# Lightning attention into a top-1 mixture of experts: token lists built on the chip by one-hot products, attention steps in three array shapes, ordered masks, and first loads by half heads

## The chip, the cores and the metric

The kernel runs on one core of a Trainium2 chip. A core has TensorE (PE, with a separate queue for its weight loads, PEld), VectorE (DVE), ScalarE (ACT), GpSimd (POOL) and SyncE (SP, which issues transfers here), an on-chip SBUF, and the matmul accumulators PSUM in eight banks. The metric is device microseconds of one execution, lower is better. Times are medians of several runs; durations inside the kernel come from one profiled execution.

## The reference

Everything is fp32. `q`, `k`, `v` have the shape (B, H, S, D) = (4, 8, 768, 64); `lam` has one decay per head. The second half has N = B x S = 3072 tokens of 512 features, E = 8 experts and F = 1024 hidden features.

```python
# attention, per 64-position block, with a state (D x D) per batch and head
intra = (q_blk @ k_blk.T) * Dmask            # Dmask[i, j] = lam ** (i - j) for i >= j, else 0
out_blk = intra @ v_blk + (q_blk * lam ** (pos + 1)) @ kv_state
kv_state = lam ** 64 * kv_state + (k_blk * lam ** (63 - pos)).T @ v_blk
...
x = out.transpose(0, 2, 1, 3).reshape(B * S, H * D)     # 3072 x 512
# top-1 mixture of experts
logits = x @ w_gate
expert = argmax(logits, axis=1)
gate = softmax probability of that expert
for e in range(E):
    xe = x[expert == e]
    out[expert == e] = gate * (relu(xe @ w1[e]) @ w2[e])
```

## The kernel before

**Attention.** The kernel uses chunks of 128 positions (NSTEP = 6 of them) in place of the 64 of the reference, which gives the same result. One step handles one chunk `n` of two batches; `order` is the list of the twelve steps, (0, 0), (0, 2), (1, 0), and so on. While a step is finished, the next one is prepared. The parts of a step are:

- `turn_q` and `turn_k` (L216, L228) transpose q and k on PE into `tq` and `tk` (the two halves s = 0 and 1 hold four heads each); ACT copies them to SBUF; DVE makes `qsT`, the q scaled for the state (L224), and POOL makes `kd`, the decayed k (L238).
- `score` (L243) multiplies k and q per head into PSUM banks `sp`; DVE multiplies them with the decay matrix into `mt` (L254).
- `attend` (L282) multiplies `mt` with v into `op`; `attend_states` (L265) adds what comes from the running state `st`, in two goes (`way` 0 and 1).
- `grow` (L296) makes the new contribution `cp` to the state; `update` (L308) adds it, after POOL has decayed the old state (`sd`, L316).
- `rows` (L320) transposes the result with identity columns and gate weights side by side (`back`) into `tx`, so that the rows of x and the gate logits come out of one product; ACT copies both, and x is written to a DRAM array `xs`.

**Routing.** `choose` (L338) takes the largest logit of each token, makes a one-hot `oh` of its expert and keeps the running counts `acc`. `put` (L370) computes with two products (`rank`) where each token stands in its expert's list, and POOL scatters an entry (row in `xs`, row in the output, gate value) for each token into a DRAM array `slots`, 128 tokens by one indirect transfer (L390, 24 in all). `slots` was filled with empty entries at the start. This is done for groups of four batches (512 tokens) for the first four chunks, and of two for the last two.

**Experts.** Expert 0 comes first, in two passes: 256 tokens gathered early ("0a", from `start_early`, L685 on) while attention still runs, then the rest ("0b"). The other seven follow in an order sorted by their counts. A pass loads its list from `slots` (L412), gathers its rows of `xs` (L436), transposes them (`tp`, L465), multiplies with w1 (`ph`, L475, or the faster form `hidden_fast`, `p`, L551) and w2 (`po`, L609, and `p`, L579), and scatters the rows to the output (L442). Weights, 2 MB of w1 and 2 MB of w2 per expert, are loaded by SP, double buffered. ACT and DVE share the copies out of PSUM: the transposed rows (`xgT`, L450 and L452), the hidden layer with its relu (`hT`), and the outputs `o`. When the early group has its counts (`acc_early`), the product `had` (L688) tells how many of expert 0's tokens there are by then, so that the places of later tokens start behind the 256 of the early pass. A small ACT copy, `fence` (L280), keeps attend from writing the `op` banks while the states' products still do.

**Order.** Where the code says `pin` (`tc.keep_in_program_order`), the instructions keep the order of the program among themselves; all other instructions are placed by the framework's scheduler. All matmuls of the steps are pinned. PSUM banks are shared: `sp`, `tq`, `tk` in 0 to 3; `cp` in 4; `rank` and `had` in 5; `op` in 6 and 7; `tx` of the first batch of a step in 4 and 5, of the second in 6 and 7. The order of PE in a step is `leave(last)` (its eight `tx` products), the turns of the next step, `rank` where a group is due, states way 0, `cp`, attend, states way 1, and the next step's scores. These are several shapes of use of the array (rows x columns): 128x128 for `tx` and turns, 64x64 for states, 128x64 for `cp` and attend, 64x128 for scores.

Of the kernel before, what the change touches and what calls it, by code (L numbers as in the profile page):

```python
# [20 lines left out]
def kernel(  # L21
# [28 lines left out]

    nc = tc.nc
# [4 lines left out]
    P = 128  # L56
# [7 lines left out]
    TG = 3  # L64
    NR = E - 1
# [5 lines left out]
    CUT = B // 2  # L71
# [10 lines left out]

    xs = dram.tile([1 + N, MD], F32, name="xs")
# [4 lines left out]

    def load(n, b0, first=False):

        got = [qkv.tile([P, 2, H, D], F32, tag=name, name=f"{name}_in") for name in "qkv"]
        per = 1 if first else 2
        for t, src in zip(got, (q, k, v)):
            queue = nc.scalar if first and src is k else nc.sync
            for b in range(0, 2, per):
                queue.dma_start(
                    out=t[:, b:b + per].rearrange("p b h d -> p (b h) d"),
                    in_=src[b0 + b:b0 + b + per, :, n * C:(n + 1) * C, :].rearrange(
                        "b h s d -> s (b h) d"))
            if first and src is q:  # L100
                load_lam()
        return got
# [3 lines left out]

    def load_lam():
        nc.sync.dma_start(out=lam_bc, in_=lam.partition_broadcast(P))

# [12 lines left out]
    for j, u in itertools.product(range(2), range(2)):  # L122
        nc.scalar.dma_start(out=back[(u ^ j) * D:((u ^ j) + 1) * D, :, P + j * E:P + (j + 1) * E],
                            in_=by_chunk[j, u])
# [21 lines left out]
    for i in range(E):  # L146
        nc.vector.memset(caps[:, i:i + 1], float(CAPS[i]))

    entry = const.tile([P, NSTEP, B, ENTRY], F32, name="entry")
    nc.gpsimd.memset(entry, 0.0)  # L150
    nc.gpsimd.iota(entry[:, :, :, 0].bitcast(I32), pattern=[[B * C, NSTEP], [C, B]], base=1,
                   channel_multiplier=1)
    nc.gpsimd.iota(entry[:, :, :, 1].bitcast(I32), pattern=[[C, NSTEP], [S, B]], base=0,
                   channel_multiplier=1)
# [23 lines left out]
    def load_weights(e):  # L178
        w1t = wpool.tile([P, DC, F], F32, tag="w1", name="w1t")
        nc.sync.dma_start(out=w1t, in_=pick(w1_r, e))  # L180
        w2t = wpool.tile([P, FC, MD], F32, tag="w2", name="w2t")
        nc.sync.dma_start(out=w2t, in_=pick(w2_r, e))
# [21 lines left out]
    def pin(inst):  # L204
        tc.keep_in_program_order(inst)


    turned_shape = [P, HP // 2, 2, C]

    def turned(src, s, t):  # L210
        for i, b in itertools.product(range(HP // 2), range(2)):
            h = s * HP + 2 * i
            pin(nc.tensor.transpose(t[:, i, b, :], src[:, b, h:h + 2, :], ident))  # L213
# [29 lines left out]
    def score(m, s):  # L243
# [3 lines left out]
        for i, b, u in itertools.product(range(HP // 2), range(2), range(2)):  # L247
            pin(nc.tensor.matmul(  # L248
                sp[u][:, i, b, :], lhsT=m.kT[s][halves[u], i, b, :], rhs=m.qT[s][halves[u], i, b, :],
                start=(i == 0 and b == 0), stop=(i == HP // 2 - 1 and b == 1),  # L250
                skip_group_check=True))
        mt = work.tile([P, 2, HP // 2, 2, C], F32, tag="mt", name="mt")
        for u in range(2):
            nc.vector.tensor_mul(  # L254
                mt[:, u], sp[u],
                decay[:, u, s * HP // 2:(s + 1) * HP // 2].unsqueeze(2).to_broadcast(shp))
        m.mt.append(mt)

    fence = const.tile([P, 1], F32, name="fence")
# [4 lines left out]

    def attend_states(m, way):  # L265

        if way == 0:
            m.op = [bank(6 + b, [P, HP, C], f"op{b}") for b in range(2)]
        if m.n > 0:
            for hp, b in itertools.product(range(HP), range(2)):  # L270
                u = b ^ way
                pin(nc.tensor.matmul(  # L272
                    out_at(m, b, u, hp), lhsT=st[halves[u], m.b + b, hp, :],
                    rhs=m.qsT[hp // 2][halves[u], hp % 2, b, :],
                    start=(way == 0 and hp < 2), stop=(way == 1 and hp >= HP - 2),
                    skip_group_check=True))
        if m.n > 0 and way == 0:


            nc.scalar.copy(fence[halves[0]], out_at(m, 1, 1, HP - 1)[:, C - 1:])  # L280

    def attend(m):  # L282
        for hp, b, u in itertools.product(range(HP), range(2), range(2)):
# [568 lines left out]
```

## Time and profile before

| what | value |
|---|---|
| median of 3 runs | 479.15 us (478.34 to 479.39) |
| profiled execution, its own time | 478.98 us |
| its span, first to last instruction | 477.2 us |
| mean granted TensorE clock | 0.997 |
| bytes moved by DMA | 72.84 MB, mean 153 GB/s |

The span has three parts. Attention with routing lasts to about 131 us, the first expert's early pass overlaps its end, and the passes of the experts fill the rest, to the last scatter. A line of the timeline view reads: start, length, engine, source line, operation, output and inputs by the program's names, shape of the array use, sizes, count, and in brackets the engine's idle time before it and what ended that. Durations of matmuls overlap, since they are pipelined, so the distance between two starts tells the cost. A line of the windows view gives the window, its length, the busy time and number of instructions of PE, PEld, DVE, ACT and POOL, the granted clock, the busy share of DMA, and the GB/s.

### The profile page before, as it was taken

Reading aid. Unit: us, or ns where it says so; the run is one execution under the profiler, and the core shown is the slowest. Engines: PE = TensorE matmul, PEld = TensorE weight load, DVE = VectorE, ACT = ScalarE, POOL = GpSimd, SP = SyncE. Lnnn points to the kernel's source line nnn. Section 1 sums busy time; section 2 is a strip of 40 time slices with the busy share of each in tenths; the row PEclk is TensorE's granted clock in tenths of the full one; section 3 lists DMA queues with packets and bytes.
Section 4 is the critical chain, followed back from the end, with each engine's and each line's share of the span. In section 5 each row is a group of like instructions: output and inputs, shape, how many; then the busy total and the mean of one; then the engine's idle time right before and its main releaser. Section 6 shows DMA issues by size and latency. Waiting matters only on the chain.

```text
span 477.2 us, 8695 instructions
## 1 busy us (share of the span) xinstructions
PE 457.3 (96%) x3468; PEld 383.1 (80%) x3468; DVE 224.4 (47%) x525; ACT 127.0 (27%) x323; POOL 247.7 (52%) x189
## 2 busy tenths in 40 slices
PE   4799999999899999999999999999999999999994
PEld 3789999998686677957994898699699689779963
DVE  3657758585450134452345436434524623753421
ACT  3364445544320111222131122113112212211310
POOL 5423644524335829849806951991694497711001
PEclk9999999999999999999999999999999999999998
DMA  9999999999318557060506152351633615001001
GB/s 170 240 243 260 217 239 216 257 305 279 101 47 320 157 193 250 32 243 33 208 13 242 36 212 87 157 199 47 243 110 132 233 39 211 0 19 44 1 17 51
DMA packets 99856, 72.84 MB, mean 153 GB/s; under 512 B 81226, under 2 KB 81230, under 8 KB 99808
## 3 DMA queue, kind: packets, MB, share of 16 engines
q1 hardware_dynamic: 88688, 51.97, 39.2%
q0 software_dynamic: 5008, 13.41, 7.8%
q10 hardware_dynamic: 6112, 6.83, 4.3%
q8 instruction: 29, 0.48, 0.5%
q14 instruction: 19, 0.16, 0.1%
HBM read 59.13 MB, written 13.40 MB: 152 GB/s over the span
## 4 chain that ended last, share of the span: by engine, by line
PE 71%; issue 3%; DVE 1%; DMA 1%; POOL 0%; POOLq 0%; ACT 0%
PE p L551 28%; PE p L579 18%; PE po L609 16%; PE ph L475 5%; PE tp L465 3%; DMA xg<-xs,list_0a 1%; DVE h_qsT L498 0%; DVE hT L560 0%; PE tx L326 0%; POOL slots L390 0%; PE tx L328 0%; DVE xgT L452 0%; PE rank L377 0%; POOLq L805 0%; ACT hT L562 0%
## 5 line engine op out<-in xcount | busy, mean ns | idle before, releaser
L609 PE MATMUL po<-w2t,hT 128*128 128x512 f32 (+2 forms) x224 | 81.1, 597 | 0.0
L436 POOL DMA_INDIRECT xg<-xs,list x24 | 26.0, 1084 | 75.7 <-PE tp L465 70.2
L609 PEld LDWEIGHTS po<-w2t,hT 128*128 128x128 f32 (+2 forms) x224 | 31.6, 169 | 37.5 <-issue 37.2
L562 ACT ACTIVATE hT<-hT 128x384 f32<-128x384 f32 (+2 forms) x56 | 30.2, 540 | 89.8 <-DVE hT L560 89.8
L442 POOL DMA_INDIRECT out_dram<-o,list x24 | 23.7, 989 | 52.0 <-DVE o L615 28.9
L551 PE MATMUL p<-xgT,w1t 128*128 128x192 f32 (+2 forms) x224 | 42.8, 334 | 0.0
L390 POOL DMA_INDIRECT slots<-entry,slot_i x24 | 23.6, 985 | 34.9 <-DVE slot_i L388 13.7
L551 PEld LDWEIGHTS p<-xgT,w1t 128*128 128x128 f32 x224 | 38.7, 190 | 1.1 <-issue 0.8
L238 POOL TENSOR_TENSOR kd<-k_in,kdec 128x512 f32<-128x512 f32 x20 | 20.4, 1042 | 26.5 <-PE cp L301 14.7
L254 DVE TENSOR_TENSOR mt<-sp,decay 128x512 f32<-128x512 f32 x48 | 29.8, 682 | 6.2 <-PE sp L248 6.1
L591 DVE SCALAR_TENSOR_TENSOR o<-p,list,o 128x256 f32<-128x256 f32 x28 | 13.5, 483 | 32.9 <-PE p L579 17.0
L579 PE MATMUL p<-w2t,hT 128*128 128x256 f32 x112 | 26.8, 382 | 0.0
L579 PEld LDWEIGHTS p<-w2t,hT 128*128 128x128 f32 x112 | 21.0, 190 | 6.9 <-issue 4.4
L248 PE MATMUL sp<-qT,kT 64*128 64x128 f32 x384 | 24.7, 278 | 0.1
L248 PEld LDWEIGHTS sp<-qT,kT 64*128 64x128 f32 x384 | 22.4, 188 | 2.2 <-issue 1.9
L284 PE MATMUL op<-mt,v_in 128*64 128x128 f32 x384 | 23.6, 274 | 0.4 <-ACT fence L280 0.4
L475 PE MATMUL ph<-xgT,w1t 128*128 128x256 f32 (+1 forms) x128 | 23.9, 342 | 0.0
L560 DVE TENSOR_TENSOR hT<-p,u_qsT 128x384 f32<-128x384 f32 (+2 forms) x28 | 16.1, 575 | 16.5 <-PE p L551 16.5
L213 PE MATMUL tq<-ident,q_in 128*128 128x128 f32 x96 | 15.4, 286 | 7.9 <-DMA q_in<-in_q_dram 6.8
L465 PEld LDWEIGHTS tp<-ident,xg 128*128 128x128 f32 (+1 forms) x112 | 13.4, 140 | 11.7 <-issue 3.6
L293 ACT COPY xT<-op 128x512 f32<-128x512 f32 x24 | 12.9, 590 | 33.6 <-PE op L272 29.8
L488 DVE TENSOR_TENSOR u_kT<-p,u_qT 128x384 f32<-128x384 f32 (+2 forms) x14 | 8.1, 576 | 29.3 <-PE p L551 29.3
(162 smaller groups left out, 968.5 us busy)
## 6 DMA issues: line engine op xcount, KB each, us to landing
w1t<-in_moe_w_dram SPq DMA_DIRECT2D x8, 2048.0 KB, 7.7
w2t<-in_moe_w_dram SPq DMA_DIRECT2D x8, 2048.0 KB, 9.1
xs<-x ACTq DMA_DIRECT2D x24, 256.0 KB, 4.8
q_in<-in_q_dram SPq DMA_DIRECT2D x11, 512.0 KB, 8.4
k_in<-in_k_dram SPq DMA_DIRECT2D x11, 512.0 KB, 8.4
v_in<-in_v_dram SPq DMA_DIRECT2D x11, 512.0 KB, 8.7
q_in<-in_q_dram SPq DMA_DIRECT2D x2, 256.0 KB, 5.9
k_in<-in_k_dram ACTq DMA_DIRECT2D x2, 256.0 KB, 5.6
```

Of the source, the lines that this page charges most:

```text
L248: pin(nc.tensor.matmul(sp[u][:, i, b, :], lhsT=m.kT[s][halves[u], i, b, :], rhs=m.qT[s][halves[u], i, b, :], start=(i == 0 and b == 0), st ...
L254: nc.vector.tensor_mul(mt[:, u], sp[u], decay[:, u, s * HP // 2:(s + 1) * HP // 2].unsqueeze(2).to_broadcast(shp))
L284: pin(nc.tensor.matmul(out_at(m, b, u, hp), lhsT=m.v[:, b, 2 * hp + u, :], rhs=m.mt[hp // 2][:, u, hp % 2, b, :], start=(m.n == 0 and hp = ...
L390: put = nc.gpsimd.indirect_dma_start(out=slots, out_offset=bass.IndirectOffsetOnAxis(ap=slot_i[:, i:i + 1], axis=0), in_=entry[:, n, b, :] ...
L436: nc.gpsimd.indirect_dma_start(out=dst, out_offset=None, in_=xs[:rows, :], in_offset=bass.IndirectOffsetOnAxis(ap=idx, axis=0))
L442: put = nc.gpsimd.indirect_dma_start(out=out, out_offset=bass.IndirectOffsetOnAxis(ap=idx, axis=0), in_=src, in_offset=None, bounds_check= ...
L465: pin(nc.tensor.transpose(tp[:, t * P:t * P + w], m.xg[t // 2][:w, t % 2, dc * P:(dc + 1) * P], ident[:w, :w]))
L475: nc.tensor.matmul(ph, lhsT=w1t[:, dc, fc * P:(fc + 1) * P], rhs=m.xgT[:, dc, :], start=(dc == 0), stop=(dc == DC - 1))
L551: nc.tensor.matmul(p[:, i, :], lhsT=lhs[:, dc, (c + i) * P:(c + i + 1) * P], rhs=rhs[:, dc, :], start=(dc == 0), stop=(dc == DH - 1))
L562: nc.scalar.activation(outs[i][k], outs[i][k], ACT.Relu)
L579: nc.tensor.matmul(p, lhsT=lhs[:, fc, :], rhs=rhs[:, fc, :], start=(fc == 0), stop=(fc == FC // 2 - 1))
L609: nc.tensor.matmul(po[part], lhsT=m.hT[:, fc, t * P:t * P + w], rhs=w2t[:, fc, :], start=(i < k), stop=(i >= FC - k), skip_group_check=True)
```

## The change

Four things are changed together.

1. **Lists on chip.** `put` becomes `place` and `fill`. `place` computes each token's spot in the lists as before (the DVE array that was called `place` is now `spots`, and reads `rank` first), then splits it into the tile of the list (spot >> 7) and the lane (spot & 127). DVE compares an iota with the lane to make a one-hot matrix `to` (128x128), and puts token row and gate into the column of the tile in `what` (128x64). `fill` multiplies the two on PE into `new` (bank 5), and DVE adds that to `lists` in SBUF. No entry is scattered to DRAM, `slots` isn't emptied at the start, and no list is loaded; row numbers for the gathers and the output are worked out by DVE in `rows_of`. The lists of the seven sorted experts are picked by products with `is_r` (`by_turn`). The scatter to `slots` is kept in a branch that runs only where an expert gets more tokens than the passes hold. Chunk 4 is now grouped by four batches too, so there are seven groups (five of 512 tokens, two of 256), and the early pass takes tokens of chunks 0 to 3.
2. **Three array shapes.** The score products are halved in columns, to 64x64. The order of PE in a step becomes: `rank` where due, turns of half 0 and `tx` of the first batch, turns of half 1 and `tx` of the second, `cp`, attend, `fill` where due, states way 0, scores, states way 1.
3. **Masks and update ordered.** The masks (`mask`, the product with the decay) and the update of the state are kept in program order on DVE: mask of half 0, update, mask of half 1. `sd` on POOL is issued ahead of `cp`.
4. **First loads.** q and k of the first step are loaded by halves of the heads, on SP and ACT; gate weights and `lam` go to POOL's queue; all loads on SP keep the program's order, with the first weights ahead of the last v.

The core of the diff:

```diff
+        if first:
+            for hs, b, i in itertools.product((slice(0, HP), slice(HP, H)), range(2), range(2)):
+                (nc.sync, nc.scalar)[i].dma_start(
+                    out=got[i][:, b, hs],
+                    in_=(q, k)[i][b0 + b, hs, where, :].rearrange("h s d -> s h d"))
...
+            if (n, b0) == (NSTEP - 1, B - 2) and src is v:
+                weights.append(load_weights(0))
...
-    def load_lam():
-        nc.sync.dma_start(out=lam_bc, in_=lam.partition_broadcast(P))
+    nc.gpsimd.dma_start(out=lam_bc, in_=lam.partition_broadcast(P))
...
-        for i, b, u in itertools.product(range(HP // 2), range(2), range(2)):
-            pin(nc.tensor.matmul(
-                sp[u][:, i, b, :], lhsT=m.kT[s][halves[u], i, b, :], rhs=m.qT[s][halves[u], i, b, :],
+        for i, b, u, keys in itertools.product(range(HP // 2), range(2), range(2), halves):
+            in_order(nc.tensor.matmul(
+                sp[u][keys, i, b, :], lhsT=m.kT[s][halves[u], i, b, keys],
+                rhs=m.qT[s][halves[u], i, b, :],
...
-        for i, b in enumerate(bs):
-            put = nc.gpsimd.indirect_dma_start(
-                out=slots, out_offset=bass.IndirectOffsetOnAxis(ap=slot_i[:, i:i + 1], axis=0),
-                in_=entry[:, n, b, :], in_offset=None)
+        nc.vector.tensor_single_scalar(parts_i[:, 0], spot, 7, op=ALU.arith_shift_right)
+        nc.vector.tensor_single_scalar(parts_i[:, 1], spot, P - 1, op=ALU.bitwise_and)
...
+            nc.vector.tensor_scalar(out=to[:, i], in0=lane, scalar1=parts[:, 1, i:i + 1],
+                                    scalar2=None, op0=ALU.is_equal)
+            nc.vector.scalar_tensor_tensor(
+                out=what[:, i],
+                in0=tiles_of.rearrange("p e t -> p (e t)").unsqueeze(2).to_broadcast(shp),
+                scalar=parts[:, 0, i:i + 1],
+                in1=entry[:, n, b].unsqueeze(1).to_broadcast(shp),
+                op0=ALU.is_equal, op1=ALU.mult)
...
+        new = bank(5, [P, E * NT * 2], "new")
+        for i, half in itertools.product(range(len(bs)), halves):
+            mm = nc.tensor.matmul(
+                new[half], lhsT=to[:, i, half], rhs=what[:, i].rearrange("p c k -> p (c k)"),
+                start=(i == 0), stop=(i == len(bs) - 1), skip_group_check=True)
...
     for i in range(len(order)):
-        due = chosen.pop() if chosen else None
-        if last:
-            leave(last)
+        give_places()
         ahead = enter(*order[i + 1]) if i + 1 < len(order) else None
...
+            for s in range(2):
+                if ahead:
+                    turn_q(ahead, s)
+                    turn_k(ahead, s)
+                leave(last, s)
+            grow(cur)
+            attend(cur)
+            fill_lists()
         attend_states(cur, 0)
-        grow(cur)
-        attend(cur)
...
         if ahead:
             for s in range(2):
                 score(ahead, s)
+            mask(ahead, 0)
+        else:
+            turn(passes[0], in_order)
+            give_places()
+        attend_states(cur, 1)
+        if i > 0:
+            to_sbuf(cur)
+            update(cur)
+        if ahead:
+            mask(ahead, 1)
```

## The prediction

> **What bounds the kernel now.** I read the head of the page first, for the busy time of each engine and the chain that ended last:
>
> ```profile
> span 477.2 us, 8695 instructions
> PE 457.3 (96%) x3468; PEld 383.1 (80%) x3468; DVE 224.4 (47%) x525; ACT 127.0 (27%) x323; POOL 247.7 (52%) x189
> PE   4799999999899999999999999999999999999994
> PE 71%; issue 3%; DVE 1%; DMA 1%; POOL 0%; POOLq 0%; ACT 0%
> ```
>
> TensorE is busy for 457.3 of 477.2 us, so it is idle for 19.9 in all: the first two slices, one place near slice 10, one of 1.05 us at 414, and the last scatter of some 6.5 us. Time changes only where PE's own work changes, or where PE waits. I therefore read PE's timeline next, in an undisturbed step (columns: start, length, operation, count):
>
> ```profile
> 62.85 0.60 PE L213 MATMUL tq<-ident,q_in 128*128 128x128 f32 x4
> 64.60 0.31 PE L377 MATMUL rank<-oh,before 128*128 128x32 f32 x2
> 65.06 0.67 PE L272 MATMUL op<-qsT,st 64*64 64x128 f32 x16
> 65.66 1.15 PE L301 MATMUL cp<-v_in,kd 128*64 128x64 f32 x32
> 66.64 1.92 PE L284 MATMUL op<-mt,v_in 128*64 128x128 f32 x32
> 68.49 0.67 PE L272 MATMUL op<-qsT,st 64*64 64x128 f32 x16
> 69.09 2.06 PE L248 MATMUL sp<-qT,kT 64*128 64x128 f32 x32
> 71.07 0.50 PE L326 MATMUL tx<-back,xT 128*128 128x136 f32 x2
> ...
> 73.03 0.60 PE L213 MATMUL tq<-ident,q_in 128*128 128x128 f32 x4
> ...
> 80.88 0.50 PE L326 MATMUL tx<-back,xT 128*128 128x136 f32 x2
> ```
>
> Starts are what to read, since ends overlap: a step takes 80.88 - 71.07 = 9.81 us, and one with a rank 71.07 - 60.90 = 10.17, together 19.98 per pair of steps. PE never pauses here. Then the same view at the start and where attention hands over to the experts, where the bracket names the wait:
>
> ```profile
> 7.23 1.76 PE L213 MATMUL tq<-ident,q_in 128*128 128x128 f32 x7 [1.94 <-DMA q_in<-in_q_dram]
> 15.75 0.63 PE L213 MATMUL tk<-ident,k_in 128*128 128x128 f32 x4 [1.45 <-DMA k_in<-in_k_dram]
> 109.34 0.39 PE L688 MATMUL had<-acc_early,ones 128*128 128x8 f32 x2 [0.27 <-DVE place L383]
> 117.25 1.75 PE L284 MATMUL op<-mt,v_in 128*64 128x128 f32 x28 [0.18 <-ACT fence L280]
> 125.65 1.75 PE L284 MATMUL op<-mt,v_in 128*64 128x128 f32 x28 [0.20 <-ACT fence L280]
> 129.53 0.55 PE L465 MATMUL tp<-ident,xg 128*128 128x128 f32 x3 [1.27 <-DMA xg<-xs,list_0a]
> ```
>
> Last the stage windows (busy PE, PEld, DVE, ACT, POOL, then clock, DMA share, GB/s), and DVE's timeline where a POOL product runs beside it:
>
> ```profile
> 0.00:20.00 20.00, 10.55 (x128) 9.35 (x128) 7.54 (x29) 5.84 (x10) 9.84 (x29) 1.00 1.07 203
> 80.00:100.00 20.00, 20.00 (x330) 18.52 (x328) 13.78 (x36) 9.82 (x32) 10.11 (x10) 1.00 1.03 282
> 96.23 0.17 DVE L367 TENSOR_TENSOR acc<-acc,oh 128x8 f32<-128x8 f32 x1
> 96.43 0.92 DVE L366 COPY ohc<-acc 128x8 f32<-128x8 f32 x1
> ```
>
> In the steps DVE is 69% busy and the transfers fill their share; in the first 20 us PE is half idle while the DMA engines are full. The 0.92 us for a copy that elsewhere takes 0.17 falls inside a `kd` product on POOL (96.28 to 97.32). All of it ran at clock 1.00, so no term below needs a clock.
>
> **The changes on PE.** From about 137 us the experts' passes are the same products; the sum concerns what lies before. Inside a block, by the raw starts of the matmuls, a transpose costs 0.109 us, a `tx` 0.2325, four 64x64 passes together 0.109, a `cp` pair 0.058, an attend pair 0.109, two score passes 0.112. A step's work is thus 8 x 0.2325 + 16 x 0.109 + 2 x 0.436 (states) + 0.933 (cp) + 1.747 (attend) + 1.787 (score) = 8.95; the other 0.86 of 9.81 are five changes of array shape. The score products are halved in columns: twice the instructions, 64 passes, four at once as the states' passes show, 16 x 0.109 = 1.74; should they be limited by the rate of issue that the `cp` stream shows (14.6 ns each, 128 instructions), 1.87. I take 1.74, since the states have the same form. Three shapes instead of five leave about 0.50 for changes (0.42 to 0.60), so a step becomes about 8.91 + 0.50 = 9.41, 0.40 less. Against this stands `fill`: two products of two passes per 128 tokens, priced by attend's passes, 0.117; a group of four 0.47. A pair of steps is then 2 x 9.41 + 0.47 + 0.36 to 0.46 (rank) = 19.65 to 19.75, or 0.30 less; over five pairs -1.5, and with one rank pair fewer at the end against two small fills, -1.6. With scores at 1.87 it is -0.2.
>
> **Waits that go.** The lists are on chip, so 24 indirect scatters on POOL (985 ns each, 23.6 us busy), the filling of the empty list (0.44 MB), and seven list loads on SP go. On PE's path that frees the gather wait: the early tokens now end one step group sooner and their gather is issued at about 112, ahead of the turn at 128. 1.27 + the two fence waits 0.38 + had's old 0.27 = -1.9. Released gathers and the first weights move past each other on SP and POOL: v of the last step is then behind 4 MB of weights and lands at some 113, needed at 123, so nothing is paid; if that cover went, each us late is a us of PE. The 0.30 for `xgT` stays, as 0.4.
>
> **The start.** q and k come in halves on two queues, so the first score can start at 7 rather than 10.5. But PE then runs into k of the second step, which needs 8 loads x 0.524 = 4.19 MB. Transfers begin at 2.1 us; the first window's 203 GB/s x 20 us is 4.06 MB in 17.9 us, 0.227 MB per us, and 4.19 MB end at 20.6, up to 1 us more for the tail (a list load of 6 KB takes 3.4 from issue to landing, so not all of a transfer is bytes). With the fullest slice's rate, 0.26, it is 18.2 + 1. The step that began at 21.99 then begins between 19.2 and 21.9: a gain of 0.1 to 2.8. I take the middle, -1.45. Gate and lam go to POOL's queue, 4 and 1 issues of 0.76 to 1.0 ahead of nothing PE waits for; lam landed at 8 before and may land there again, the first masks need it.
>
> **Waits that come.** New on DVE per four groups: three small steps 3 x 0.20, four `to` (128x128: between 128x32 at 0.19 and 128x512 at 0.68, 0.29) and four `what` (0.22), one add to the lists 0.20: 2.2 to 2.8. DVE goes from 13.8 to some 16.3 of 20 us: room on average, so order decides.
> First, `spots` reads rank's bank 5, and `tx` of the first batch needs that bank. Let T be the end of the first score half. PE: second half and states, 0.87 + 0.44; rank 0.46; tq, tk 0.875; `tx` on bank 4 0.465: it wants bank 5 at T + 3.1. DVE: 0.2 for release, mask 2 x 0.60, update 0.60, mask 2 x 0.60, `spots` 0.2, release 0.1: T + 3.5. So 0.35 to 0.4 in each rank step (0 if DVE gains on PE, 0.95 if the chain of choose is held up by two `kd` as at 96.43 and the first mask is 0.6 late). Three such steps and 0.2 at the end: +1.25. Behind the waiting `tx` on PE stand that step's second turns and everything else.
> Second, at the early group `had` follows rank at once in bank 5 and waits from T + 1.8 to T + 3.4: +1.6 (0.3 as before, to 2.2).
> Third, the last two steps have no `cp` or no turns between `tx` of the second batch and attend, which write the same banks 6 and 7: attend waits for ACT's copies, 2 x (0.06 + 0.26) and their release, 0.3 to 0.75 each: +0.8. `xgT` +0.1.
>
> [...]
>
> [...]
>
> **Sum.** -1.6 - 1.9 - 1.45 + 1.25 + 1.6 + 0.8 + 0.1 = -1.2 on the profiled execution's 478.98 us (span 477.2 and 1.8 around it), which is 0.17 below the median of 479.15. Against the median: 477.9.
>
> **Rivals.** *DVE's order becomes the bound.* Every rank step pays 0.95 + 0.6, `had` 2.2, attend 1.5, and scores 1.87: -0.2 - 1.9 - 0.7 + 4.7 + 2.2 + 1.5 + 0.1 = +5.7; with scores at 1.74, +4.3, about 483. For it: 16.3 of 20 us, and masks now pinned ahead of everything; against it: PSUM-fed work was never held up. It decides once the first mask starts more than about 0.5 us after T.
> *The start gives all.* PE is never held at k, -2.8, and DVE keeps up (tx 0, had 0.3, attend 0.6): -1.6 - 1.9 - 2.8 + 1.0 = -5.3, 473.7. For it: full DMA slices reach 0.26 to 0.30; against: the first window's 0.227.
> *The start gives nothing,* because bytes set it anyway, and the rest is as summed: +0.2, 479.3.
> *Scores do not run four at once,* 64 passes in pairs: +1.74 for each of 11, 497. The states' rows speak against it.
>
> **Numbers.** Forecast 0.40, large gain 0.27, slow DVE 0.19, no gain at the start 0.12, scores in pairs 0.02. About 0.2%, 0.96 us, is the least that this kernel's runs can tell from no change. Of the forecast 0.26 falls beyond it, 0.11 within, 0.03 slower; with the large gain that makes faster 0.53; same 0.11 + 0.09 = 0.20; slower 0.03 + 0.03 + 0.21 = 0.27. The range, 473.4 to 482.6, leaves out the pairs, half of the slow case's far end and the last of the large gain's.
>
> **What would show it.** Score blocks 1.74 to 1.87 apart at 64*64; pairs of steps 19.7 to 20.1 between `tx` starts, with a bracket of 0.3 to 0.4 on `tx` naming DVE `spots`; `had` 1.6; no bracket on `tp<-ident,xg`; first score near 7; the second step's first `tk` waiting for k till 20 to 21.6; the first `po` near 147 instead of 148.08. Pairs above 20.5 mean the DVE rival, a `po` under 143.5 the large gain.

## The result, and the profile after

The changed kernel takes 484.27 us (483.75 to 487.26, 4 runs) against 479.27 for the kernel before: ratio 1.0120, 95% interval 1.0076 to 1.0165. Taken once more in a later comparison, it was 484.37 against 477.50: 1.0143 (1.0121 to 1.0165). It is slower by about 1.2 to 1.4%, where 0.25% faster was forecast. The profiled execution took 484.77, its span is 482.6.

First the head of the page after, as it was read before:

```profile
span 482.6 us, 9686 instructions
PE 464.1 (96%) x3944; PEld 389.7 (81%) x3944; DVE 239.7 (50%) x621; ACT 126.7 (26%) x322; POOL 225.6 (47%) x168
PEclk9999999989999999999999999999999999999999
PE 84%; DVE 6%; ACT 3%; DMA 2%; SPq 2%; issue 1%; ACTq 0%; POOLq 0%; POOL 0%; DVEq 0%
```

PE is busy for 6.8 us longer, more than the products of `fill` explain (3.6 by the distances between starts: five of 0.56 to 0.57, two of 0.38 and 0.39), and one slice of its granted clock is an 8: the same work ran slower somewhere. Where, PE's timeline rows tell (start, length, operation, count, and in brackets the wait):

```profile
23.42 0.63 PE L221 MATMUL tk<-ident,k_in 128*128 128x128 f32 x4 [0.38 <-DMA k_in<-in_k_dram]
38.93 1.93 PE L256 MATMUL sp<-qT,kT 64*64 64x128 f32 x64
62.04 0.45 PE L291 MATMUL op<-qsT,st 64*64 64x128 f32 x7 [0.27 <-issue]
64.65 0.50 PE L337 MATMUL tx<-back,xT 128*128 128x136 f32 x2 [0.23 <-DVE spots L394]
70.89 1.93 PE L256 MATMUL sp<-qT,kT 64*64 64x128 f32 x64
80.45 1.93 PE L256 MATMUL sp<-qT,kT 64*64 64x128 f32 x64
91.23 1.93 PE L256 MATMUL sp<-qT,kT 64*64 64x128 f32 x64
100.78 1.94 PE L256 MATMUL sp<-qT,kT 64*64 64x128 f32 x64
105.33 0.59 PE L733 MATMUL had<-acc_early,ones 128*128 128x8 f32 x2 [1.61 <-DVE spots L394]
105.78 1.09 PE L221 MATMUL tq<-ident,q_in 128*128 128x128 f32 x4
114.72 1.71 PE L256 MATMUL sp<-qT,kT 64*64 64x128 f32 x54
130.20 2.10 PE L281 MATMUL op<-mt,v_in 128*64 128x128 f32 x32 [0.44 <-ACT x L344]
153.38 3.17 PE L654 MATMUL po<-w2t,hT 128*128 128x512 f32 x7
```

Scores of the same step are the marks by which the two kernels can be laid side by side. Their starts, and the first `po`:

| mark | before | after | late by | added since the last mark |
|---|---|---|---|---|
| scores of chunk 1, second pair of batches | 38.93 | 38.93 | 0.00 | 0.00 |
| chunk 3, first pair | 69.09 | 70.89 | 1.80 | 1.80 |
| chunk 4, second pair | 98.88 | 100.78 | 1.90 | 0.10 |
| chunk 5, first pair | 110.25 | 114.72 | 4.47 | 2.57 |
| chunk 5, second pair | 119.53 | 124.38 | 4.85 | 0.38 |
| first `po` | 147.92 | 153.38 | 5.46 | 0.61 |
| end of the span | 477.2 | 482.6 | 5.4 | -0.1 |

All of the loss lies before the first `po`; the experts' passes are the same to 0.1 us. The largest piece is the step of the early group. The windows view shows why it is more than its wait of 1.61 us (the columns end with clock, DMA share and GB/s):

```profile
104.00:106.00 2.00, 0.67 (x3) 0.67 (x4) 1.50 (x5) 0.30 (x1) 0.00 (x0) 0.83 1.01 403
106.00:108.00 2.00, 2.00 (x11) 2.00 (x11) 1.93 (x14) 0.82 (x2) 0.00 (x0) 0.50 1.04 394
108.00:110.00 2.00, 2.00 (x16) 2.00 (x16) 1.19 (x5) 1.23 (x5) 0.00 (x0) 0.82 1.05 393
```

TensorE was granted half its clock from 105.30 to 108.72, and the four `tq` at 105.78 take 0.89 to the next row's start where they otherwise take 0.44. DVE's timeline shows what the wait was for: `spots` behind the second mask, as forecast.

```profile
103.30 0.69 DVE L329 TENSOR_TENSOR st<-cp,sd 128x512 f32<-128x512 f32 x1
103.91 1.28 DVE L267 TENSOR_TENSOR mt<-sp,decay 128x512 f32<-128x512 f32 x2
105.10 0.18 DVE L394 TENSOR_TENSOR spots<-rank,ebase 128x32 f32<-128x32 f32 x1
```

### The profile page after: what moved, and what is told of

Read it like the earlier page. It is cut to its first block, busy times and chain, and to the rows that moved or that the text cites. A ratio compares the mean times of both kernels' runs of the same rounds, so it can differ in the third digit from the quotient of the medians.

```text
span 482.6 us, 9686 instructions
## 1 busy us (share of the span) xinstructions
PE 464.1 (96%) x3944; PEld 389.7 (81%) x3944; DVE 239.7 (50%) x621; ACT 126.7 (26%) x322; POOL 225.6 (47%) x168
## 4 chain that ended last, share of the span: by engine, by line
PE 84%; DVE 6%; ACT 3%; DMA 2%; SPq 2%; issue 1%; ACTq 0%; POOLq 0%; POOL 0%; DVEq 0%
PE p L596 27%; PE p L624 18%; PE po L654 16%; PE ph L520 5%; PE tp L509 3%; PE op L281 3%; PE sp L256 3%; DMA k_in<-in_k_dram 2%; SPq L107 2%; PE tx L337 2%; PE op L291 2%; DVE mt L267 2%; PE tx L339 1%; PE cp L316 1%; PE tk L221 1%; PE tq L221 1%
## 5 line engine op out<-in xcount | busy, mean ns | idle before, releaser
L480 POOL DMA_INDIRECT xg<-xs,ids_r x24 | 26.0, 1082 | 77.8 <-PE tp L509 71.5
L486 POOL DMA_INDIRECT out_dram<-o,ids_r x24 | 23.8, 991 | 52.1 <-DVE o L660 28.9
L246 POOL TENSOR_TENSOR kd<-k_in,kdec 128x512 f32<-128x512 f32 x20 | 20.5, 1044 | 34.0 <-issue 21.6
L636 DVE SCALAR_TENSOR_TENSOR o<-p,by_turn,o 128x256 f32<-128x256 f32 x28 | 13.5, 483 | 32.9 <-PE p L624 17.0
L256 PE MATMUL sp<-qT,kT 64*64 64x128 f32 x768 | 25.7, 283 | 2.0 <-ACT kT L240 1.8
L256 PEld LDWEIGHTS sp<-qT,kT 64*64 64x64 f32 x768 | 22.9, 140 | 3.4 <-ACT kT L240 2.8
L281 PE MATMUL op<-mt,v_in 128*64 128x128 f32 x384 | 23.4, 274 | 0.7 <-ACT x L344 0.7
L311 POOL TENSOR_TENSOR sd<-st,sdec 128x512 f32<-128x512 f32 x8 | 8.3, 1040 | 29.2 <-DVE st L329 12.4
L281 PEld LDWEIGHTS op<-mt,v_in 128*64 128x64 f32 x384 | 20.7, 137 | 1.6 <-ACT x L344 1.1
L520 PEld LDWEIGHTS ph<-xgT,w1t 128*128 128x128 f32 x128 | 20.5, 190 | 1.8 <-issue 0.2
```

The costliest lines, as they stand in the source:

```text
L246: nc.gpsimd.tensor_tensor(out=kd, in0=m.k[:, :, hs], in1=kdec[:, hs].unsqueeze(1).unsqueeze(3).to_broadcast(shp), op=ALU.mult)
L256: in_order(nc.tensor.matmul(sp[u][keys, i, b, :], lhsT=m.kT[s][halves[u], i, b, keys], rhs=m.qT[s][halves[u], i, b, :], start=(i == 0 and ...
L281: in_order(nc.tensor.matmul(out_at(m, b, u, hp), lhsT=m.v[:, b, 2 * hp + u, :], rhs=m.mt[hp // 2][:, u, hp % 2, b, :], start=(hp == 0), st ...
L480: nc.gpsimd.indirect_dma_start(out=dst, out_offset=None, in_=xs[:rows, :], in_offset=bass.IndirectOffsetOnAxis(ap=idx, axis=0))
L486: put = nc.gpsimd.indirect_dma_start(out=out, out_offset=bass.IndirectOffsetOnAxis(ap=idx, axis=0), in_=src, in_offset=None, bounds_check= ...
L520: in_order(nc.tensor.matmul(ph, lhsT=w1t[:, dc, fc * P:(fc + 1) * P], rhs=m.xgT[:, dc, :], start=(dc == 0), stop=(dc == DC - 1)))
```

## The experiments

Ratios are to the kernel before on the same chip in the same comparison. The kernel before took 480.05 and 480.16 us in two comparisons on one chip (experiments 1 to 8, the small shift excepted), 477.50 on a second chip (experiment 11) and 487.71 on a third (experiments 9 and 10, and the small shift), so only ratios and trace rows are compared between them.

### 1. The start: turns before scores

```diff
     for s in range(2):
         turn_q(cur, s)
         turn_k(cur, s)
+    for s in range(2):
         score(cur, s)
         mask(cur, s)
```

> The changed kernel, with the first step's turns all made before its first scores (q, k, q, k by halves, then both scores), so that the two waits of scores for ACT's copy of k (0.68 us at 7.2, 0.67 at 11.8) go. Theory A, the half clock sets the start: TensorE ran at half speed until 16.56 us in the changed kernel and until 9.96 before; without the waits it is at full speed by about 10, and what ran at half speed after that (some 6 us) takes 2.5 to 3 less: about 481.5. Rival B, k of the second step sets the start by its bytes: the clock is full by about 10 all the same, but the bracket on that k grows from 0.4 to some 3 us, its tk still starts near 23.4, and the time is 483.8 to 484.3.

Measured: 485.46, ratio 1.0098 (1.0062 to 1.0134). In its profile the clock is full from 12.75 on, not 16.56, and PE's timeline says:

```profile
23.21 0.63 PE L221 MATMUL tk<-ident,k_in 128*128 128x128 f32 x4 [1.68 <-DMA k_in<-in_k_dram]
63.27 0.45 PE L291 MATMUL op<-qsT,st 64*64 64x128 f32 x7 [1.72 <-issue]
```

What PE gained it waits out at k of the second step, whose `tk` starts at 23.21 as against 23.42. By its rows that is rival B: the early first scores and the slow clock at the start cost nothing, since k of the second step comes no sooner. The time is 1.2 above rival B's: in this profile the pause of the second row was followed by a half clock from 63.95 to 67.36, and the wait of `had` by another from 108.32 to 111.73. The load of that k left SP's queue at the same moment in both kernels (SP's timeline, before and after; start and length of the issue):

```profile
16.46 2.32 SPq L96 DMA_DIRECT2D k_in<-in_k_dram  x1
14.96 3.76 SPq L107 DMA_DIRECT2D k_in<-in_k_dram  x1
```

16.46 + 2.32 = 18.78 and 14.96 + 3.76 = 18.72. It was put in earlier and held longer. The pause of 1.72 us named "issue" (PE stands still and waits for nothing that the profile shows) is taken up in the experiments on instructions.

### 2. had beside rank

```diff
-        rank = bank(5, shp, "rank")
+        whole_rank = bank(5, [P, nb + early_now, E], "rank")
+        rank = whole_rank[:, :nb]
...
+        if early_now:
+            skip_places(whole_rank[:, nb])     # the product had, no bank of its own
```

> The changed kernel, with the counts of the early group (had) written beside rank in the same PSUM tile, so that had no longer waits for DVE to read rank. Theory A: the wait of 1.61 us goes, and with it the half clock from 105.30 to 108.72 that followed; the work in that stretch takes 1.6 less at full speed: 1.6 + 1.6 = 3.2 less, about 481.1. Rival B: the clock falls for another reason (the little work of rank and had in that stretch); then only the wait goes, 482.7. Rival C: what is saved is given back behind it (a later wait for a gather or for weights): 484.

Measured: 482.69, ratio 1.0060 (1.0035 to 1.0086) against 1.0120 and 1.0143: 2.9 to 4.0 us less by the ratios, as theory A said. The bare time is rival B's 482.7, but on this chip the kernel before is 0.8 slower than at first, and experiments 1 and 7, which keep the wait, took 485.46 and 485.94 on it. The median granted clock of their runs is 0.992, here it is 0.997. The wait is gone, the clock of the profile stays full there, and only a rest is left:

```profile
105.66 0.47 PE L337 MATMUL tx<-back,xT 128*128 128x136 f32 x2 [0.18 <-DVE skip L742]
```

The distance of scores around it falls from 13.94 to 10.91.

### 3. Undivided scores

```diff
-        for i, b, u, keys in itertools.product(range(HP // 2), range(2), range(2), halves):
-            in_order(nc.tensor.matmul(sp[u][keys, i, b, :], lhsT=m.kT[s][halves[u], i, b, keys],
+        for i, b, u in itertools.product(range(HP // 2), range(2), range(2)):
+            in_order(nc.tensor.matmul(sp[u][:, i, b, :], lhsT=m.kT[s][halves[u], i, b, :],
```

> The changed kernel with the scores undivided (64x128, half as many matmuls), all else as changed. Theory A: the quarter shape is worth its two saved changes of shape; undivided, the score block takes about 1.79 instead of 1.75 and two changes of 0.15 to 0.2 come back, 0.35 per step, 11 steps: +3.5 to +4, about 488. Rival B: the doubled count of instructions costs what the shape gives, and the two pauses of PE marked issue (near 61 and 116, about 0.45 each) come from it: they vanish, and the time is 484 to 486. For the start: if narrow array use is what kept the clock low until 16.56, it is full by about 10 here; if the waits did it, it stays low until 13 to 17.

Measured: 485.51, ratio 1.0113 (1.0074 to 1.0152), on the same chip as experiment 1 with 485.46. Its steps are longer as expected, 9.95 without rank instead of 9.55, 11.2 with it instead of 10.78. Yet the total did not rise, and no row of its PE timeline has a pause named "issue". That is rival B. Its clock is full from 11.09 with the same waits as the changed kernel's; but experiment 2, with waits and shapes as in the changed kernel, had it from 11.68 instead of 16.56, so that moment varies by execution and tells nothing of the shape. Also here had waited 1.61 us (at 107.62), and the clock did not fall.

### 4. Three shapes with the lists in DRAM

The kernel before, with the order and shapes of the changed one; the grouping of chunk 4, the early pass from chunks 0 to 3, and `had` beside rank come with it. Its core:

```diff
-        attend_states(cur, 0)
-        grow(cur)
-        attend(cur)
...
+        for s in range(2):
+            if ahead:
+                turn_q(ahead, s)
+                turn_k(ahead, s)
+            if i > 1:
+                leave(last, s)
+        if due:
+            give_places(due)
+        grow(cur)
+        attend(cur)
+        attend_states(cur, 0)
+        if ahead:
+            for s in range(2):
+                score(ahead, s)            # quartered
+            mask(ahead, 0)                 # pinned, as update and mask 1 behind it
+        attend_states(cur, 1)
```

> The kernel before, with its lists in DRAM and its first loads, but the order of three shapes, quartered scores, ordered masks, the regrouping of the fifth chunk and an early pass from chunks 0 to 3 (had beside rank, rank behind the tx products). Theory A: a step without rank goes from 9.81 to about 9.5, one with rank by as much, ten steps: -2.6 to -3.1; one rank pair fewer -0.4; the wait of 1.27 for the early gather goes: about 475. Rival B: the three shapes are not worth it by themselves (copies by ACT and the ordered masks bring waits of 0.2 to 0.4 per step): 478 to 481, and the loss of the changed kernel isn't due to the lists.

Measured: 485.08, ratio 1.0098 (1.0067 to 1.0129): rival B, and worse than it said. Undisturbed steps are shorter, 9.55 without rank, and 9.95 with it (10.34 less a pause of 0.39), 19.50 a pair against 19.98. But its PE timeline has pauses of 0.39 and 1.40 named "issue", 1.46 for k of the third step, and this, with ACT's row ahead of it:

```profile
99.54 0.39 ACTq L342 DMA_DIRECT2D xs<-x  x1
100.95 2.80 PE L289 MATMUL op<-mt,v_in 128*64 128x128 f32 x32 [2.38 <-ACT x L339]
```

ACT ran nothing from 96.9 to 99.5, and the copies that `attend` waits for came after the writing of a row block; that this write held them is read from the order of ACT's queue, and no run shows it. In the old order attend starts 4.0 us after the last `tx` (62.62 to 66.64), in the new one it is due 1.3 after it (87.12 to 88.43 in the changed kernel), so such a stop is no longer covered. A half clock from 102.18 to 105.59 followed. With the steps of the changed kernel this prices the lists, as an estimate from these rows: 10.78 - 9.95 = 0.83 us per group for `fill`, the changes of shape around it and around `rank`, and the wait for `spots`.

### 5. tx first in the second step

Experiment 2 with all `tx` of the second step ahead of its turns (`if i == 1: leave(last, 0); leave(last, 1)`).

> The changed kernel with had beside rank, as in the run of that name (482.7), and in the second step alone all eight tx products ahead of the turns. So far k of the second step let its tk start at 23.21 to 23.58 whatever stood before it. Theory A, bytes and the order of work set the start: the 1.96 us of tx are done while PE waits (1.72 in that run), the next scores start near 27.5 instead of 29.4, and the time falls by 1.5 to 1.9, to 481. Rival B: the transfers behind are late by as much, the bracket turns up at k of the third step (near 32), and the time stays 482 to 483.

Measured: 482.19, ratio 1.0051 (1.0033 to 1.0070), 0.5 us below experiment 2: rival B.

```profile
32.75 0.63 PE L221 MATMUL tk<-ident,k_in 128*128 128x128 f32 x4 [1.15 <-DVE mt L267]
```

The scores of the second step start at 28.79 instead of 29.36, and then k of the third step is waited for (the row names a mask, DVE's, that had long ended; in experiment 4 and in the small shift below the same place names `k_in`, with 1.46 and 1.49). The third step's scores begin at 40.01, where experiment 2 has 38.75: the gain is gone, to that wait and a pause of 0.34 at 38.72.

### 6. The program shifted

Experiment 5 with 32 idle products of zeros ahead of the first transpose (128 columns by 64), and in a second run of 32 columns by one.

> The kernel of the run beside it (tx first in the second step), with 32 idle products of zeros on PE before the first transpose, while PE waits for q. They add about 128 instructions, half of one of the 16 KB fetches that bring PE its program, and do nothing else. Theory A, the pauses of PE marked issue come from a fetch that ends too late in the dense scores: they move to other steps than the ones near 62 and 114, by about half the distance between two fetches (3 us), or vanish. Rival B, something else in those two steps makes them: they stay there. Of the time theory A says only that it moves by up to 1.5 either way; the clock should also be full earlier, which by the runs so far is worth nothing at the start.

Measured: 490.71, ratio 1.0238 (1.0198 to 1.0278), since the idle products took 13.9 us and put the scores off by 5 to 7; of their cost the expectation was wrong. The pauses moved. In experiment 5 they are at 38.72, 62.93 and 114.75; here at 66.03, 109.13 and 118.23. The ones in the 60s, there and here:

```profile
62.93 0.45 PE L291 MATMUL op<-qsT,st 64*64 64x128 f32 x8 [0.44 <-issue]
66.03 1.76 PE L256 MATMUL sp<-qT,kT 64*64 64x128 f32 x56 [0.19 <-issue]
```

Counted from the scores they follow, the one in the 60s moved from 2.58 to 0.59 after the scores' start, the last from 2.13 after it to 0.28 ahead of it: 2.0 and 2.4 us earlier in the program. That is theory A.

> The kernel with had beside rank and tx first in the second step (482.2), with 32 idle products ahead of the first transpose as in the run that shifted the program, but of 32 columns and one moving column, so that they end before q lands or soon after (their predecessors took 13.9 us). Theory A: pauses marked issue move from the places in that kernel's profile (38.7, 62.9, 114.8) to those where the shifted run had them, some 3 us earlier in the program, each 0.2 to 0.3 instead of 0.3 to 0.4: 481 to 482. Rival B, pauses stay at 38, 63 and 114.

Measured: 484.26 on the chip where the kernel before took 487.71, ratio 0.9938 (0.9912 to 0.9965). PE's timeline:

```profile
52.85 0.43 PE L291 MATMUL op<-qsT,st 64*64 64x128 f32 x3 [0.66 <-issue]
104.02 0.38 PE L291 MATMUL op<-qsT,st 64*64 64x128 f32 x2 [0.53 <-issue]
113.13 0.54 PE L291 MATMUL op<-qsT,st 64*64 64x128 f32 x10 [0.26 <-issue]
115.33 0.45 PE L256 MATMUL sp<-qT,kT 64*64 64x128 f32 x5 [0.29 <-issue]
```

The two at 104.02 and 113.13 are where the first shifted run had them (2.89 after and 0.28 before the scores' start; there 2.59 and 0.28), none is left near 63, the third of the first shifted run (66.03) has no counterpart, those at 52.85 and from 115.33 on are new, and the sizes were not as expected. So the pauses go with the place in the program, not with the step; whether one comes at its place varies (experiment 7). That the ratio is below 1 here, and 1.0051 without the shift on another chip, is not explained by the shift: the changed order unpinned stood at 1.0034 on this chip too, with far longer steps. A part is the clock. The runs of the kernel before have a median granted clock of 0.991 here, against 0.996 and 0.997 on the other chips, and those of the small shift 0.996: (1 - 0.991) x 486 = 4.4 us lost to the clock (an estimate) against 1.9.

### 7. First loads by whole heads

```diff
-            for hs, b, i in itertools.product((slice(0, HP), slice(HP, H)), range(2), range(2)):
+            for b, i in itertools.product(range(2), range(2)):
```

> The changed kernel, with the first q and k loaded by whole heads (256 KB each) on the same two queues. Theory A, the second step's k sets the start: the first score starts 1 to 2 us later, tk of the second step still at 23.2 to 23.6, and the time is that of the changed kernel, 484. Rival B, the early first score is worth what it is early: 485.5 to 486.

Measured: 485.94, ratio 1.0135 (1.0092 to 1.0177); the interval holds the changed kernel's ratio. First scores at 9.75 instead of 7.22, `tk` of the second step at 23.81 instead of 23.42: 2.5 us at the first score are 0.4 two steps on. By the rows that is theory A; the bare time is rival B's, and the interval alone would not exclude it. This profile has no pause named "issue", though PE's program is that of the changed kernel.

### 8. The kernel before with the early pass one group sooner

Chunk 4 in one group, `early = groups[NSTEP - 3]`, had beside rank; all else as before.

> The kernel before in all but the groups: the fifth chunk in one group of four batches, the early pass from chunks 0 to 3, had beside rank. Theory A, the handover's wait of 1.27 for the gather and one rank pair (0.4) are all that this saves: 477 to 477.5, 0.4% less than before. Rival B: the list and the gather are early, but PE then waits for something as late, the weights or a copy: no change.

Measured: 479.40, ratio 0.9992 (0.9958 to 1.0026): rival B.

```profile
125.10 0.99 POOL L440 DMA_INDIRECT xg<-xs,list_0a  x1 [12.97 <-issue]
130.03 1.60 PE L469 MATMUL tp<-ident,xg 128*128 128x128 f32 x5 [1.20 <-DMA xg<-xs,list_0a]
```

The gather is issued at 125.10 against 124.40 before. The last scatter of the group was issued at 111.15, and the load of the list left SP from 118.28 to 121.45. (In this profile TensorE was at half clock from 130.16 to 136.99, behind that wait and one of 0.76 ahead of it; it took 482.44, the median is 479.40.) Regrouping alone does not make a list in DRAM early; having it on chip did (no wait for `xg` in any profile of the changed kernel).

### 9. Masks and update not ordered

`in_order` taken off the masks and the update.

> The changed kernel without the order of masks and update on DVE (the scheduler places them). Theory A: the order costs what stands behind the masks, the wait of had (1.61, with a half clock after it in three of four profiles) and those of tx for spots (0.24 to 0.5 in each rank step); free, DVE takes spots first, and the time falls by 1 to 3 us, to 481.5 to 483. Rival B: the scheduler puts them in nearly the same order, or a late mask or update makes PE wait at attend or at the states instead: 484 or more.

Measured: 489.09, ratio 1.0034 (1.0009 to 1.0058), on the chip where the kernel before took 487.71. The ratio agrees with theory A, the trace does not:

```profile
98.75 0.68 DVE L329 TENSOR_TENSOR st<-cp,sd 128x512 f32<-128x512 f32 x1
99.58 0.47 PE L337 MATMUL tx<-back,xT 128*128 128x136 f32 x2 [0.93 <-DVE st L329]
```

Without the order the scheduler puts the update behind all four masks, `tx` waits for bank 4, and a pair of steps takes 10.53 + 11.04 = 21.57 us instead of 20.33. had's wait is still 1.52. By its rows the order of masks is worth 1.2 us a pair. Why the ratio is low on this chip stays open.

### 10. Rows written later

Experiment 4 with the two writes of a step's rows issued together behind all copies.

> The kernel with lists in DRAM and three shapes (485.1), with the two writes of rows of a step issued together behind all of its copies. In that kernel's profile one such write held ACT's queue from 96.9 to 99.5, the copies behind it made attend wait 2.38 us, and a half clock of 3.41 us followed. Theory A, those are accidents of the queue: wait and half clock go, 3 to 4 us, to 481 to 482, and the pauses marked issue remain (0.4 to 1.4 each). Rival B: the write holds up other copies instead (the fence or xT), 484 to 485.

Measured: 501.31, ratio 1.0287 (1.0250 to 1.0324). Both theories fall. PE stood still all along the steps, in waits named "issue":

```profile
123.09 0.44 PE L248 MATMUL sp<-qT,kT 64*64 64x128 f32 x5 [0.29 <-issue]
123.81 0.45 PE L248 MATMUL sp<-qT,kT 64*64 64x128 f32 x5 [0.28 <-issue]
124.56 0.45 PE L248 MATMUL sp<-qT,kT 64*64 64x128 f32 x5 [0.29 <-issue]
```

A few products, then some 0.3 us of nothing. The same kernel with its writes as in experiment 4 was not run on this chip, so the two aren't separated. The record speaks for the chip: such trains, 0.7 to 0.8 us from one to the next, are in all three profiles taken there (in experiment 9 at 119.66, 120.42 and 121.17, in the small shift at 115.33 and 116.06) and in none from the others. The clock was lower too, 0.982 in the median, with three half clocks up to 156 us.

### 11. On one chip: the changed kernel, rank later, and rank later with undivided scores

The two variants also have `had` beside rank and, in the second step, tx first, as in experiment 5. The core of what is new:

```diff
             for s in range(2):
                 if ahead:
                     turn_q(ahead, s)
                     turn_k(ahead, s)
+                if s and due:
+                    give_places(due)
                 leave(last, s)
             grow(cur)
             attend(cur)
-            fill_lists()
+            fill_lists(ready)        # groups placed in earlier steps only
```

> The changed kernel itself, on the same chip and against the same runs of the kernel before as the two beside it. In the last comparison the kernel before took 487.7 instead of 479 to 480, on another chip, and the unpinned variant, whose steps are 1.2 us per pair longer in the trace, stood only 0.3% behind it. Theory A: the loss is in the kernel, ratio 1.010 to 1.015 again, with had's wait of 1.61 and its half clock in most executions. Rival B: part of the 1.2% is the chip, ratio 1.003 to 1.008.

> The changed kernel with had beside rank, rank put between the second turns and the second tx products of a step (so no tx waits for spots), fill one pair of steps' half later (after the next step's attend), and tx first in the second step. Theory A: the waits for spots (0.24 to 0.5 in three steps) and had's (1.61 and half clock) go, a pair of steps takes 19.95 to 20.05 instead of 20.33, 1 to 1.3 less than with had beside rank and tx first alone (ratio 1.005): 1.002 to 1.003. The pauses marked issue remain. Rival B: DVE is now late elsewhere (the place chain in the second half of the step delays masks), pairs stay at 20.3 or more: 1.005 or above.

> The kernel beside it with undivided scores, 384 matmuls fewer. Theory A, the doubled instructions of the scores cost what their shape gives: steps 0.4 longer (4.4 in eleven), no pause marked issue, no half clock, so that the time is within 0.3% of the kernel beside it, and its runs lie closer together. Rival B, the pauses are small beside the shape's gain: 0.6 to 0.9% slower than the kernel beside it.

Measured, against 477.50: the changed kernel 484.37, ratio 1.0143 (1.0121 to 1.0165); rank later 481.90, 1.0082 (1.0064 to 1.0100); rank later and scores undivided 484.26, 1.0132 (1.0111 to 1.0153).

The loss is in the kernel (theory A of the first). The edits of rank later together save 2.5 us, less than expected; its ratio is rival B's, its pair of steps lies between the two. Since experiment 5, without the later rank, stood at 1.0051, moving rank isn't shown to save anything. At the end of attention it has waits of 0.70, 0.53 and 0.68 where experiment 5 has 0.44 and 0.30. With neither wait left, its steps read:

```profile
79.25 1.93 PE L256 MATMUL sp<-qT,kT 64*64 64x128 f32 x64
84.48 0.41 PE L390 MATMUL rank<-oh,before 128*128 128x32 f32 x2
89.37 1.93 PE L256 MATMUL sp<-qT,kT 64*64 64x128 f32 x64
98.34 0.63 PE L428 MATMUL new<-what,to 128*64 128x64 f32 x16
99.39 1.98 PE L256 MATMUL sp<-qT,kT 64*64 64x128 f32 x63
```

89.37 - 79.25 = 10.12 with rank and 99.39 - 89.37 = 10.02 with `fill`: 20.14 a pair and not a wait in it, against 19.98 before. The undivided scores make a pair 20.94, no pause is named "issue", and the runs lie within 0.9 us. 0.80 a pair is 4.4 over eleven steps, but the time is only 2.4 longer; the pauses that the quartered kernel's profile names are 0.47 + 0.41 + 0.53 = 1.4 of the other 2.0, and a pause costs more than its bracket (the step with the one of 0.41 took 10.76, its like without one 10.12). The quartered shape earns about half of what its steps show, between the two theories.

The run of the changed kernel also gave a comparison that no edit could: its profile has had's wait of 1.61 and no fall of the clock (the row names a load, which `had` doesn't read; `spots` is what it waits for, as before):

```profile
105.37 0.39 PE L733 MATMUL had<-acc_early,ones 128*128 128x8 f32 x2 [1.61 <-DMA w1t<-in_moe_w_dram]
```

The scores on both sides lie 12.30 apart; 13.94 and 13.97 where the clock fell (the first profile and experiment 7). The half clock costs 1.64 to 1.67 us. It followed a wait of 1.61 in three of five profiles (the first, experiments 1 and 7; not in experiment 3 and here).

## Why the prediction was wrong, point by point

- **"No term below needs a clock" failed.** It cost 1.65 us where had waits, in some executions. The stretch of 0.50 lasts 3.4 us, from 105.30 to 108.72; those of experiment 1 (63.95 to 67.36 and 108.32 to 111.73) and of experiment 4 (102.18 to 105.59) are as long, that of experiment 8 lasts 6.8 (130.16 to 136.99). What starts one is not shown: behind the same 1.61 us of waiting it came in three profiles and stayed away in two. The prediction also read the clock column, 1.00, at the start; the rows speak otherwise: seven `tq` from 7.23 to 8.77 are 0.22 each, twice the 0.11 that they take from 62.85 on. That error cost nothing, as experiment 1 showed.
- **The start (-1.45) was worth 0.** The step named was right (PE runs into the second step's k), the rate was not: k came at 23.4, where 20 to 21.6 was forecast. The scores behind it start 0.42 later than before (29.54, before 29.12), and the next step, in the new order, makes that good. A mean of bytes over a window doesn't tell when a load in order leaves its queue: at 18.7 in both kernels.
- **The shapes (-1.5 over five pairs) were mis-sized.** A step without rank takes 9.55, not 9.41: changes of shape sum to 0.65, not 0.50. The rank step's extra over it, less the wait for `spots` (0.24), is 10.78 - 9.55 - 0.24 = 0.99, not 0.83 to 0.93. A pair without waits is 20.09, 0.11 more than before instead of 0.30 less. With the fills at the end, 0.57, 0.38 and 0.39 between starts where a gain of 0.1 net was put in, and with the old waits and the new ones taken out, the term comes to +1.3 instead of -1.6.
- **"Scores at 1.74" was right** (1.75 in undisturbed blocks: 38.93 to 40.68), and the price lay elsewhere: in the pauses named "issue", which no term had: two cost 1.2 in this profile.
- **Waits that go:** the gather's 1.27 went, as summed. **Waits that come:** `spots` 0.50, 0.23 and 0.24 for 1.25 with 0.2 at the end; had 1.61 for 1.6; attend 0.25 + 0.44 for 0.8. These were right, with their releasers.
- **The rival of DVE's order** gave about 483, near the result, for a reason that did not occur: at the early group the first mask starts at 102.03, 0.4 us after the first half of its scores (100.78 + 0.87), below the 0.5 that was set as this rival's sign; DVE is behind only where it was forecast to be. What spoke against it held: the 48 masks, which read the PSUM banks `sp`, took 0.68 to 0.69 each in both kernels, also beside POOL (before, four from 40.20 on with `sd` from 40.36 to 41.40). Its number is no proof of it.

In the sum, by the profiles: the start missed its forecast by 1.45, shapes with fills by 2.9; the half clock took 1.65, two pauses 1.2 (0.58 where the step from 59.53 took 11.36 instead of 10.78, 0.59 where that from 114.72 took 9.66 instead of the 9.07 of experiment 1); the new waits came out 0.5 smaller than summed. That is 6.7, from -1.2 to +5.5 (so much later is the first `po`; the medians are 5.0 apart).

Open is why the comparison on the chip with 487.71 turned out as it did, but for the part of the clock. No version here is shown to be better than the kernel before: experiment 8 is level, and the small shift was ahead on that chip only.

## What to carry to other kernels

Before a gain on a busy engine is summed, ask of three things that the busy share doesn't show: when the next load in order leaves its queue (here at 18.7 in both kernels, so that the earlier first scores earned nothing), whether a half clock can follow a new wait (behind had's 1.61 us one did in three of five profiles, for 1.64 to 1.67), and how many instructions per microsecond the denser form needs (here 192 in 2.8 us, with pauses of 0.21 to 1.72). Read the clock from the distance of rows as well as from its column (0.22 for a `tq` under a column of 1.00, where later ones took 0.11). Place a product whose PSUM bank a slow reader holds so that other products, in other banks, stand between it and the next use of that bank (with rank later no `tx` waits for `spots` in the steps shown, where the changed kernel waited 0.50, 0.23 and 0.24).

## What the runs showed of the hardware that was not expected

PE stood still in these runs for what looks like its own program: its pauses named "issue" go with packets of a queue that the page's DMA part calls "instruction". Its line, before and after:

```profile
q8 instruction: 29, 0.48, 0.5%
q8 instruction: 33, 0.54, 0.5%
```

Four packets of 16 KB more for 476 matmuls and 476 weight loads more are about 69 bytes for each instruction (an estimate from these rows), so a packet holds some 240, and scores with the states around them are 192 in 2.8 us. In the changed kernel a packet was under way from 59.32 to 60.60 and PE went on at 62.04. Five profiles have the same number of PE instructions ahead of two such places; there the pause grows with the time by which the packet ends late, counted from the start of the scores (us):

| profile | scores near 59: packet ends | pause | scores near 114: packet ends | pause |
|---|---|---|---|---|
| experiment 7 | 0.27 after | none | 0.21 ahead | none |
| changed kernel | 1.06 after | 0.27 | 0.53 after | 0.21 |
| changed kernel, experiment 11 | 1.24 after | 0.35 | 1.24 after | 0.86 |
| experiment 2 | 1.50 after | 0.62 | 1.21 after | 0.77 |
| experiment 1 | 2.45 after | 1.72 | 0.11 ahead | none |

All 18 pauses named "issue" ahead of the first `po`, in all profiles but the three from the chip with 487.71, end 1.25 to 1.54 us after a packet's end. The pauses are absent from both profiles with undivided scores in the new order (experiments 3 and 11) and move with the program (6). So the late packet is the cause as far as traces can tell; why a packet starts late in one execution and not in another stays open, and so do the trains of experiment 10, which stand at no fixed distance from a packet.

The new DVE operations on SBUF could take longer beside POOL, as the copy of the row at 96.43 did (0.92 for 0.17): with rank later, `to` took 1.03 and `what` 1.07 at 86.98 and 87.93, while `kd` ran from 86.88 to 88.92, and 0.27 right after. In no profile of the changed kernel does a product of `fill` wait for them.
